# Linear attention with a relu-squared network behind it: other places in the period for the last attention group of even periods, and for some steps of odd and even periods

## Chip, core and metric

The kernel runs on one core of a Trainium2 chip. The metric is the device time of one execution in microseconds (us); of several runs the median counts. The matmul engine is TensorE (PE, its weight loads PEld), the others are VectorE (DVE), ScalarE (ACT) and GpSimd (POOL); SyncE (SP) issues the DMAs.

## What is computed

The input has 4 batches of 8 heads, 768 steps and 48 dimensions. Per head a delta rule runs over the steps, and the 8 heads side by side then pass a two-layer network:

```python
for t in range(S):
    kt, vt, bt = (k_n[:, :, t], v[:, :, t], beta[:, :, t, None])
    y[:, :, t] = np.einsum('bhd,bhde->bhe', q[:, :, t], state)
    v_old = np.einsum('bhde,bhd->bhe', state, kt)
    state = state + bt[:, :, :, None] * np.einsum('bhd,bhe->bhde', kt, vt - v_old)
...
x = np.ascontiguousarray(attn_out.transpose(0, 2, 1, 3)).reshape(B * S, H * D)
h = np.maximum(x @ w_in, 0.0)
return (h * h @ w_out)
```

`k_n` is k divided by its norm; `w_in` is 384 x 2048 and `w_out` 2048 x 384. All is float32.

## The kernel before

The 768 steps are cut into 12 units of 64 (`units`), for all 32 heads at once. Within a unit the recurrence becomes matmuls: products of the keys, the inverse of a triangular matrix of 32 x 32 (`invert`, 31 steps on DVE of two instructions each, L505 and L507), and products with the state that one unit hands to the next. The inverse is made for two units at a time, a pair. The network (`moe`) of unit u - 1 runs while the attention of unit u does; such a stretch is a period, here numbered by u. In the trace, periods 1 to 11 follow a prologue of some 100 us, in which the weights are loaded and split into a high and a low part; after period 11 comes the rest of the last network.

What PE does in a period, by lines:

- the network: 16 groups of nine matmuls of the first layer (L751, tile h), and 16 groups of six of the second (L735, tile o), with three transposes twice ahead of them (L711). After two groups of L751, ACT takes the relu, the square and a rounded copy (L758, L759, L761), and DVE takes the rest of that rounding (L726, tile h_l), which the L735 of the same columns read two steps later.
- `key_products` (L403): only in odd periods, for the next pair. ACT and DVE copy the result out (L415, L418, L420) by the letters of `copies`, per pair: A is ACT, D is DVE, B is both. `prepare` on DVE follows (L438 to L480, with POOL's L450 and L451 between), then the first steps of `invert`.
- `state_part` and `query_products`: L661 with L623 behind it; then L671 with L677; then L689 with L696, the period's last group. ACT copies w out of L677's result (L680), and L689 and L696 read w. POOL masks the result of L623 (L629). After L696, ACT copies y (L699), which the next period's L711 read.
- `below_both`: only in even periods, L593 with L594, then L605 with L606. They read what DVE makes of the finished inverse (`ended`: L525, L530, L532).

A matmul instruction of attention with float32 operands stands in the trace as two: 32 in the program are x64 in the trace.

The order is written out by hand. In each period `weave` takes the pieces of all these generators, each with a place from 0 to 1 out of the table `A`, sorts them by place and lets each issue its instructions, which every engine then runs in that order. `steps` places the attention groups (in even periods: L661, L593, L605, L671, L689; in odd ones: L403, L661, L671, L689), `inverse`, `ended` and `prepare` place DVE's work, `keys`, `queries`, `values` and `rows` place DMA loads and what follows each of them. The 31 pieces of the network stand evenly between `m0` and `m1`, and the rest of the last network's pieces (`end`, `out`) begins the next period. `first` is the number of inverse steps in an odd period; the rest falls to the even one. Tables under a period's number (2, 6, 8, 10) replace single rows of the even table for that period. And where two attention groups would touch, a piece of the network is drawn between them, while the period still has one:

```python
            gen, quiet = order.pop(0)
            if quiet is False and not apart and (filler[0], None) in order:
                order.remove((filler[0], None))
                next(filler[0], None)
            next(gen, None)
            if quiet is not True:
                apart = quiet is None
```

Of the kernel before, what the change touches and what calls it, by code (L numbers as in the profile page):

```python
# [20 lines left out]
def kernel(  # L21
# [43 lines left out]
     10: {'steps': [0.277, 0.4012, 0.4602, 0.5125, 0.5471]},  # L65
     'abs': 35,
     'ahead': 13,
     'copies': {0: 'AADA', 1: 'AADD', 2: 'ABDD'},
     'e0': 6,
     'e1': 2,  # L70
     'early': [0, 0],
     'even': {'end': 0.0,
              'ended': [0.2208, 0.2284, 0.2344, 0.2744],
              'inverse': [0.0404, 0.2141],
              'keys': [0.3956, 0.4523],
              'm0': 0.0,
              'm1': 0.5432,
              'out': 0.1098,
              'queries': [0.4923, 0.7603],
              'rows': [0.9979],  # L80
              'steps': [0.277, 0.4212, 0.4802, 0.5325, 0.5671],
              'values': [0.0128, 0.6834]},
     'f0': 0,
     'fill': [0, 0, 3, 0, 0, 1, 2, 0, 0, 1, 0, 0, 0, 0, 0, 0, 1, 0, 0, 2, 0, 0, 0, 1, 0, 0, 0, 0, 0, 0, 0, 0, 1, 0, 0, 0, 0,
              0, 0, 0, 1, 0, 0, 6, 5, 2, 1, 3, 5, 2, 3],
     'first': 11,
     'first1': 10,
     'kk': 0,
     'last': [2, 1],
     'low': 3,  # L90
     'mode': 'tttttttttttttttdd',
     'odd': {'end': 0.0,
             'inverse': [0.4412, 0.881],
             'keys': [0.0236, 0.172],
             'm0': 0.0,
             'm1': 0.8088,
             'out': 0.4224,
             'prepare': [0.3136, 0.3577],
             'queries': [0.4506, 0.8586],
             'rows': [0.9393],  # L100
             'steps': [0.2904, 0.4345, 0.7374, 0.8997],
             'values': [0.5395000000000001, 0.7395]},
     'order': '-01TABABAPPl2PBPPxPPPIIIGyZIIIIIIIIIIIIeeeecccVbbss',
     'over': 3,
     'plain': [('k', 3)]}
# [378 lines left out]
    def invert(d):  # L484
        need(("prepared", d["pair"]))
        lt, z = d["lt"], d["z"]
        if d["pair"] < FAST:
            lt = d["l16"]
            z = z.rearrange("p s t -> p (s t)")[:, :HB * QB].rearrange("p (h s t) -> p h s t", h=2, s=QB)
            tmp_ = apool.tile([P, 256], F32, name="tmp")  # L490
            for s in range(QB - 1):
                nj, nt = s + 1, QB - 1 - s
                tmp = tmp_[:, :2 * nj * nt].rearrange("p (h j t) -> p h j t", h=2, t=nt)
                nc.vector.tensor_tensor(out=tmp, op=ALU.mult, in0=lt[:, :, s:s + 1, s + 1:].broadcast_to([P, 2, nj, nt]),
                                        in1=z[:, :, :nj, s:s + 1].broadcast_to([P, 2, nj, nt]))
                nc.vector.tensor_tensor(out=z[:, :, :nj, s + 1:], in0=z[:, :, :nj, s + 1:], in1=tmp, op=ALU.subtract)
                if s == QB - 2:
                    done.add(("inverted", d["pair"]))
                yield
            return  # L500
        tmp_ = apool.tile([P, 256], F32, name="tmp")
        for s in range(HB - 1):
            nj, nt = s + 1, HB - 1 - s
            tmp = tmp_[:, :nj * nt].rearrange("p (j t) -> p j t", t=nt)
            nc.vector.tensor_tensor(out=tmp, op=ALU.mult, in0=lt[:, s:s + 1, s + 1:].broadcast_to([P, nj, nt]),  # L505
                                    in1=z[:, :nj, s:s + 1].broadcast_to([P, nj, nt]))
            nc.vector.tensor_tensor(out=z[:, :nj, s + 1:], in0=z[:, :nj, s + 1:], in1=tmp, op=ALU.subtract)  # L507
            if s == HB - 2:
                done.add(("inverted", d["pair"]))
            yield  # L510
# [363 lines left out]
    with tc.manual_schedule(engines=engines):  # L874
# [41 lines left out]
        inverse = invert(pair0)  # L916
# [16 lines left out]
        for u in range(1, A.get("stop", units)):  # L933
# [18 lines left out]
            if u % 2:  # L952
                kk = [iter(())] * 2
                if nxt:
                    inverse = invert(nxt)
# [47 lines left out]
```

## Time and profile before

| | us |
|---|---|
| median of 3 runs | 620.88 (619.26 to 621.07) |
| the profiled execution's own time | 621.46 |
| its span, first to last instruction | 619.4 |
| PE busy | 579.1 |
| DVE busy | 421.7 |
| ACT busy | 321.6 |
| POOL busy | 51.4 |

The profile is that of one execution. Busy time counts instructions, not waits; the ends of matmuls are modelled, so that the starts tell more than the ends. A wait is written behind the instruction that ended it, with who released it; "issue" is a wait for nothing that the profile shows. The chain of waits is the work that ended last, followed back from the end. A row of order of time gives start, duration, engine, line, tiles and count; a row of a stretch gives its bounds, its length and the busy time of each engine with its instructions, then the granted share of PE's clock.

### The profile page before, as it was taken

How to read it: one execution, taken by the hardware profiler on the slowest of the kernel's cores; microseconds unless marked ns; L12 is line 12 of the kernel's file. 1: busy time of each engine (PE TensorE's matmuls, PEld its weight loads, DVE VectorE, ACT ScalarE, POOL GpSimd, SP SyncE). 2: the span in 40 equal slices, each digit the busy share in tenths (PEclk: the TensorE clock that was granted, in tenths of full speed). 3: DMA queues.
4: the chain of work that ended last, by engine and by line, in shares of the span. 5: the costliest groups of instructions: out<-in, count | busy, mean ns of one | idle time of the engine just before them, and what ended most of it. 6: DMA issues, size and time to landing. Idle time of an engine off the chain costs nothing.

```text
span 619.4 us, 23429 instructions
## 1 busy us (share of the span) xinstructions
PE 579.1 (93%) x10616; PEld 550.5 (89%) x10616; DVE 421.7 (68%) x758; ACT 321.6 (52%) x507; POOL 51.4 (8%) x62
## 2 busy tenths in 40 slices
PE   5077899999999999999999999999999999999997
PEld 5055678999989999999999999999999999999997
DVE  3975989999934989845989557989349897412111
ACT  4345868645455545546544655454655455454442
POOL 3110000110100200200201001102002002001000
PEclk9568999999999999999999999999999999999999
DMA  8996070005025114045041243060252140110101
GB/s 250 273 282 197 6 124 7 4 1 93 14 41 90 31 29 76 5 70 87 3 83 23 28 80 53 3 104 3 38 82 40 28 79 3 29 27 2 28 1 25
DMA packets 146675, 37.79 MB, mean 61 GB/s; under 512 B 140272, under 2 KB 143344, under 8 KB 146576
## 3 DMA queue, kind: packets, MB, share of 16 engines
q1 hardware_dynamic: 146496, 36.20, 28.7%
q8 instruction: 83, 1.36, 0.9%
q14 instruction: 16, 0.13, 0.1%
q10 hardware_dynamic: 80, 0.10, 0.0%
HBM read 31.56 MB, written 4.72 MB: 59 GB/s over the span
## 4 chain that ended last, share of the span: by engine, by line
PE 84%; DVE 4%; SPq 4%; DMA 3%; issue 2%; ACT 2%; ACTq 0%
PE h L751 31%; PE o L735 29%; SPq L211 2%; PE o L237 2%; PE g L735 2%; PE g L237 2%; SPq L320 2%; PE g L671 2%; PE g L696 2%; PE g L677 2%; DMA kb<-in_q_dram 2%; PE g L661 2%; PE g L403 2%; PE g L623 2%; PE g L689 1%
## 5 line engine op out<-in xcount | busy, mean ns | idle before, releaser
L735 PE MATMUL o<-w,h_h 128*128 128x384 f32 x704 | 185.4, 344 | 0.0
L751 PE MATMUL h<-x_h,w 128*128 128x256 f32 x1152 | 170.3, 283 | 0.6 <-ACT x_h L713 0.6
L751 PEld LDWEIGHTS h<-x_h,w 128*128 128x128 f32 x1152 | 154.7, 190 | 1.5 <-ACT x_h L713 0.8
L726 DVE TENSOR_TENSOR h_l<-r,h_h 128x512 fp32r<-128x512 f32 x96 | 65.2, 684 | 102.1 <-ACT h_h L761 102.1
L735 PEld LDWEIGHTS o<-w,h_h 128*128 128x128 f32 x704 | 121.4, 189 | 2.7 <-issue 0.7
L758 ACT ACTIVATE r<-h 128x512 f32<-128x512 f32 x96 | 57.4, 598 | 120.7 <-PE h L751 102.2
L735 PE MATMUL o<-w,h_l 128*128 128x384 f32 x352 | 118.3, 336 | 0.0
L751 PE MATMUL h<-x_l,w 128*128 128x256 f32 x576 | 100.1, 283 | 0.0
L751 PEld LDWEIGHTS h<-x_l,w 128*128 128x128 f32 x576 | 82.5, 191 | 0.0
L735 PEld LDWEIGHTS o<-w,h_l 128*128 128x128 f32 x352 | 66.1, 188 | 0.0
L759 ACT ACTIVATE r<-r 128x512 f32<-128x512 f32 x96 | 60.8, 633 | 3.1
L761 ACT CAST h_h<-r 128x512 fp32r<-128x512 f32 x96 | 59.6, 621 | 3.0
L507 DVE TENSOR_TENSOR z<-z,tmp 128x31 f32<-128x31 f32 (+15 forms) x155 | 53.1, 343 | 5.3
L505 DVE TENSOR_TENSOR tmp<-lt,z 128x31 f32<-128x31 f32 (+15 forms) x155 | 52.5, 339 | 3.7
L629 POOL TENSOR_SCALAR_AFFINE_SELECT ap<-ap 64x1024 f32<-64x1024 f32 x24 | 32.7, 1364 | 246.5 <-ACT ap L626 227.9
L692 DVE TENSOR_TENSOR state<-state,g 48x768 f32<-48x768 f32 x22 | 20.9, 950 | 18.2 <-PE g L689 18.0
L699 ACT COPY y<-g 128x768 f32<-128x768 f32 x12 | 9.6, 799 | 40.2 <-PE g L696 40.2
L450 POOL MEMSET z<- 128x1024 f32 x5 | 4.8, 959 | 245.3 <-DVE lt L438 245.3
L714 DVE TENSOR_TENSOR x_l<-h,x_h 128x384 fp32r<-128x384 f32 x24 | 13.4, 557 | 13.7 <-ACT x_h L713 13.3
L713 ACT CAST x_h<-h 128x384 fp32r<-128x384 f32 x24 | 11.5, 479 | 20.1 <-PE h L711 20.1
L371 PE MATMUL g<-eye,tt 128*128 128x128 f32 x16 | 3.9, 424 | 17.5 <-DMA tt<-in_k_dram 16.3
L371 PEld LDWEIGHTS g<-eye,tt 128*128 128x128 f32 x16 | 3.1, 222 | 18.0 <-issue 16.4
(160 smaller groups left out, 804.0 us busy)
## 6 DMA issues: line engine op xcount, KB each, us to landing
w<-in_moe_w_out_dram SPq DMA_DIRECT2D x8, 768.0 KB, 8.4
w<-in_moe_w_in_dram SPq DMA_DIRECT2D x6, 768.0 KB, 6.8
vt<-in_v_dram SPq DMA_DIRECT2D x48, 96.0 KB, 3.2
kp<-in_k_dram SPq DMA_DIRECT2D x48, 96.0 KB, 3.3
out_dram<-rest SPq DMA_DIRECT2D x47, 96.0 KB, 2.2
kb<-in_q_dram SPq DMA_DIRECT2D x40, 64.0 KB, 2.7
kb<-in_k_dram SPq DMA_DIRECT2D x32, 64.0 KB, 2.8
w<-in_moe_w_in_dram SPq DMA_DIRECT2D x3, 512.0 KB, 8.3
```

Source lines behind the costliest of these rows:

```text
L237: nc.tensor.matmul(ps[:, c], lhsT=i, rhs=z.rearrange("p (c n) -> p c n", c=2)[:, c], start=(m == 0), stop=(m == len(terms) - 1))
L505: nc.vector.tensor_tensor(out=tmp, op=ALU.mult, in0=lt[:, s:s + 1, s + 1:].broadcast_to([P, nj, nt]), in1=z[:, :nj, s:s + 1].broadcast_to( ...
L507: nc.vector.tensor_tensor(out=z[:, :nj, s + 1:], in0=z[:, :nj, s + 1:], in1=tmp, op=ALU.subtract)
L629: nc.gpsimd.affine_select(out=half, in_=half, pattern=[[0, 2 * X], [1, C]], base=0, channel_multiplier=-1, compare_op=ALU.is_gt, fill=0.0)
L692: nc.vector.tensor_tensor(out=s[dims(j)], in0=s[dims(j)], in1=ps[dims(j)], op=ALU.add)
L714: nc.vector.tensor_tensor(out=x_l[:, :, cols], in0=xt, in1=x_h[:, :, cols].bitcast(F32), op=ALU.subtract)
L726: nc.vector.tensor_tensor(out=h_l, in0=r, in1=h_h.bitcast(F32), op=ALU.subtract)
L735: nc.tensor.matmul(o[i], lhsT=a[:, e, i * P:(i + 1) * P], rhs=w_[w], start=(ft == 0 and n == 0), stop=(ft == FT - 1 and n == 2))
L751: nc.tensor.matmul(hp[:, e], lhsT=half_of(("wi", kt, part))[w][:, f], rhs=x[:, kt], start=(n == 0), stop=(n == 3 * KT - 1))
L758: nc.scalar.activation(out=r, in_=hp, func=AF.Relu)
L759: nc.scalar.activation(out=r, in_=r, func=AF.Square)
L761: nc.scalar.copy(out=h_h, in_=r)
```

## The change

Only numbers of the table `A` change. The core of the diff, without the rows whose order in the program is shown below or stays as it was:

```diff
-     'copies': {0: 'AADA', 1: 'AADD', 2: 'ABDD'},
+     'copies': {0: 'AAAA', 1: 'AADD', 2: 'AADD'},
...
-              'm1': 0.5432,
+              'm1': 0.5244,
...
-              'steps': [0.277, 0.4212, 0.4802, 0.5325, 0.5671],
+              'steps': [0.2753, 0.398, 0.457, 0.5093, 0.6681],
...
-     'first': 11,
+     'first': 12,
...
-             'steps': [0.2904, 0.4345, 0.7374, 0.8997],
-             'values': [0.5395000000000001, 0.7395]},
+             'steps': [0.3088, 0.5641, 0.7558, 0.9181],
+             'values': [0.2314, 0.4823]},
```

The number 0.6681 for the last group of even periods holds for period 4 alone, since periods 2, 6, 8 and 10 have `steps` of their own, which stay. In period 4 no piece of the network is left to stand at the added distance, and the order on PE around that group stays: L677, six L735, L689. What does move PE's work in the other even periods is `m1`, which draws the network's pieces forward past places that stay.

In the order of PE, in period 6 from the end of L606 to the last group, before:

```order
L735 MATMUL o<-w_1267,h_l 128x384
L671 MATMUL g<-state,qt 64x48 x32
L677 MATMUL g<-vt,tt 64x48 x32
L735 MATMUL o<-w_1418,h_h 128x384 x2
L735 MATMUL o<-w_1418,h_l 128x384
L735 MATMUL o<-w_1418,h_h 128x384 x2
L735 MATMUL o<-w_1418,h_l 128x384
L689 MATMUL g<-w,kp 48x48 x32
L696 MATMUL g<-w,ap 64x48 x32
```

The same place now:

```order
L735 MATMUL o<-w_1267,h_l 128x384
L735 MATMUL o<-w_1418,h_h 128x384 x2
L735 MATMUL o<-w_1418,h_l 128x384
L735 MATMUL o<-w_1418,h_h 128x384 x2
L735 MATMUL o<-w_1418,h_l 128x384
L671 MATMUL g<-state,qt 64x48 x32
L677 MATMUL g<-vt,tt 64x48 x32
L689 MATMUL g<-w,kp 48x48 x32
L696 MATMUL g<-w,ap 64x48 x32
```

The six L735 with w_1418 moved ahead of L671, and L689 follows L677 directly. Period 8 has the same change.

In the order of PE, in period 10 at the same group, before:

```order
L671 MATMUL g<-state,qt 64x48 x32
L677 MATMUL g<-vt,tt 64x48 x32
L735 MATMUL o<-w_1267,h_h 128x384 x2
L735 MATMUL o<-w_1267,h_l 128x384
L735 MATMUL o<-w_1267,h_h 128x384 x2
L735 MATMUL o<-w_1267,h_l 128x384
L735 MATMUL o<-w_1418,h_h 128x384 x2
L735 MATMUL o<-w_1418,h_l 128x384
L735 MATMUL o<-w_1418,h_h 128x384 x2
L735 MATMUL o<-w_1418,h_l 128x384
L689 MATMUL g<-w,kp 48x48 x32
```

The same place now:

```order
L735 MATMUL o<-w_1267,h_h 128x384 x2
L735 MATMUL o<-w_1267,h_l 128x384
L671 MATMUL g<-state,qt 64x48 x32
L677 MATMUL g<-vt,tt 64x48 x32
L735 MATMUL o<-w_1418,h_h 128x384 x2
L735 MATMUL o<-w_1418,h_l 128x384
L735 MATMUL o<-w_1418,h_h 128x384 x2
L735 MATMUL o<-w_1418,h_l 128x384
L689 MATMUL g<-w,kp 48x48 x32
```

One group of six L735 (w_1267) moved from behind L677 to ahead of L671; the other six stay.

In the order of PE, in period 8 at the end of the first-layer group ahead of L593, before:

```order
L751 MATMUL h<-x_l,w_1285 128x256
L751 MATMUL h<-x_l,w_1314 128x256
L751 MATMUL h<-x_l,w_1347 128x256
L593 MATMUL g<-tt,mt 32x32
L594 MATMUL g<-t_6567,mt 32x32
```

The same place now:

```order
L751 MATMUL h<-x_l,w_1347 128x256
L751 MATMUL h<-x_h,w_1285 128x256
L751 MATMUL h<-x_h,w_1314 128x256
L751 MATMUL h<-x_h,w_1347 128x256
L751 MATMUL h<-x_h,w_1285 128x256
L751 MATMUL h<-x_h,w_1314 128x256
L751 MATMUL h<-x_h,w_1347 128x256
L751 MATMUL h<-x_l,w_1285 128x256
L751 MATMUL h<-x_l,w_1314 128x256
L751 MATMUL h<-x_l,w_1347 128x256
L593 MATMUL g<-tt,mt 32x32
L594 MATMUL g<-t_6564,mt 32x32
```

One group of nine L751 more stands ahead of L593. Period 10 has the same change, in period 6 L593 comes one group of L735 later, and in period 4 it comes one group earlier.

In odd periods 3, 5, 7 and 9, L403 comes one group of L751 later, L661 with L623 come five groups later, L671 with L677 one group later, so that twelve L735 instead of eighteen stand between L677 and L689. The loads of v and the DVE step behind them (L644) come earlier in odd periods; in periods 4, 6 and 8 the loads of k and q and the transposes behind them (L382) come some three to four groups earlier. Of the copies behind L403, the two on ACT and two on DVE of letter B (L415) become three on ACT (L418, L420) in these periods, and in the first pair three copies (L418, L420) go from DVE to ACT. Each odd period has one step of the inverse (L505, L507) more on DVE, each even one from period 4 on one less.

More of the change, by code (lines that the diff above doesn't have):

```diff
@@ L71 @@
      'early': [0, 0],
[L72 to L76, printed above, removed]
-              'm1': 0.5432,
+     'even': {'end': 0.0348,
+              'ended': [0.2238, 0.2284, 0.2612, 0.2744],
+              'inverse': [0.0457, 0.2194],
+              'keys': [0.3243, 0.3832],
+              'm0': 0.0062,
+              'm1': 0.5244,
               'out': 0.1098,
-              'queries': [0.4923, 0.7603],
+              'queries': [0.4108, 0.7603],
               'rows': [0.9979],
-              'steps': [0.277, 0.4212, 0.4802, 0.5325, 0.5671],
+              'steps': [0.2753, 0.398, 0.457, 0.5093, 0.6681],
               'values': [0.0128, 0.6834]},
@@ L91 @@
      'mode': 'tttttttttttttttdd',
-     'odd': {'end': 0.0,
-             'inverse': [0.4412, 0.881],
-             'keys': [0.0236, 0.172],
+     'odd': {'end': 0.0022,
+             'inverse': [0.4563, 0.881],
+             'keys': [0.0776, 0.172],
              'm0': 0.0,
@@ L98 @@
              'prepare': [0.3136, 0.3577],
-             'queries': [0.4506, 0.8586],
+             'queries': [0.4445, 0.8789],
              'rows': [0.9393],
-             'steps': [0.2904, 0.4345, 0.7374, 0.8997],
-             'values': [0.5395000000000001, 0.7395]},
+             'steps': [0.3088, 0.5641, 0.7558, 0.9181],
+             'values': [0.2314, 0.4823]},
      'order': '-01TABABAPPl2PBPPxPPPIIIGyZIIIIIIIIIIIIeeeecccVbbss',
```

## Prediction

> **What bounds the kernel now.** The page first, for the span and the engines' totals; then busy time by stretches; then who kept the matmul engine waiting; then the matmul engine's own order of time at the places that the change touches. The table by stretches has the time of each, then the busy time of PE, PEld, DVE, ACT and POOL with their instructions.
>
> ```profile
> span 619.4 us, 23429 instructions
> ...
> PE 579.1 (93%) x10616; PEld 550.5 (89%) x10616; DVE 421.7 (68%) x758; ACT 321.6 (52%) x507; POOL 51.4 (8%) x62
> ...
> 140.00:575.00 435.00, 432.65 (x7961) 420.51 (x7960) 302.14 (x550) 222.78 (x349) 36.85 (x28) 1.00 0.27 44
> ```
>
> From 140 to 575 us, in periods 2 to 11, PE is busy 432.65 of 435.00 us at full clock. What other engines gain there is worth nothing unless PE waits for it; what adds a wait to PE, or takes one away, is worth just that. Of its waits after the first 105 us, these are where the change reaches, with total, times and longest:
>
> ```profile
> PE g L696 <- issue: 1.4, 4, 0.5
> ...
> PE g L594 <- DVE t L532: 0.5, 2, 0.2
> ```
>
> The first row is the even periods' last group; "issue" means that no semaphore held PE. Here is period 6 from L677 on, then the break in periods 8 and 10, and an odd period's group without one:
>
> ```profile
> 355.09 1.11 PE L677 MATMUL g<-vt,tt 64*64 64x48 f32 x64
> 356.13 0.62 PE L735 MATMUL o<-w,h_h 128*128 128x384 f32 x2
> ...
> 357.38 0.94 PE L689 MATMUL g<-w,kp 64*48 64x48 f32 x64
> 358.13 0.69 PE L696 MATMUL g<-w,ap 64*64 64x48 f32 x33
> 359.04 0.68 PE L696 MATMUL g<-w,ap 64*64 64x48 f32 x31 [0.22 <-issue]
> 359.65 0.62 PE L735 MATMUL o<-w,h_h 128*128 128x384 f32 x2
> ...
> 444.20 0.62 PE L735 MATMUL o<-w,h_h 128*128 128x384 f32 x2
> ...
> 446.21 0.88 PE L696 MATMUL g<-w,ap 64*64 64x48 f32 x48
> 447.62 0.45 PE L696 MATMUL g<-w,ap 64*64 64x48 f32 x16 [0.53 <-issue]
> 448.00 0.62 PE L735 MATMUL o<-w,h_h 128*128 128x384 f32 x2
> ...
> 530.50 1.11 PE L677 MATMUL g<-vt,tt 64*64 64x48 f32 x64
> ...
> 534.59 1.11 PE L696 MATMUL g<-w,ap 64*64 64x48 f32 x63
> 536.14 0.20 PE L696 MATMUL g<-w,ap 64*64 64x48 f32 x1 [0.45 <-issue]
> 536.27 0.62 PE L735 MATMUL o<-w,h_h 128*128 128x384 f32 x2
> ...
> 401.89 1.11 PE L696 MATMUL g<-w,ap 64*64 64x48 f32 x64
> 402.94 0.45 PE L735 MATMUL o<-w,h_h 128*128 128x384 f32 x1
> ```
>
> Starts tell the cost, since the ends of matmuls are modelled. L696 takes 402.94 - 401.89 = 1.05 us undisturbed, and 1.52, 1.79 and 1.68 in periods 6, 8 and 10: breaks of 0.47, 0.74 and 0.63 us, after the 33rd, 48th and 63rd matmul. That regular step says what they are. Queue and stretches from break to break:
>
> ```profile
> q8 instruction: 83, 1.36, 0.9%
> ...
> 359.04:447.62 88.58, 87.81 (x1659) 85.31 (x1659) 65.61 (x120) 45.30 (x71) 7.86 (x6) 1.00 0.29 47
> 447.62:536.14 88.52, 87.84 (x1659) 85.19 (x1659) 64.09 (x118) 45.30 (x71) 8.14 (x6) 1.00 0.25 43
> ```
>
> 83 packets of 16 KB carry PE's 2 x 10616 instructions: a packet, a block of code, is 256 of them, or 128 matmuls with their weights. From break to break there are 1659 matmuls both times; 13 blocks are 1664, and the queue's waits fill the rest. So the breaks stand at block ends: the next block is not there yet. A block ends 128 matmuls after the last. In period 6 that is 33 of L696, 64 of L689, six of L735 and 25 of L677, so it began at about 356.13 - 25 x 0.016 = 355.7 us and the next came 3.3 us later; in period 8 (48 + 64 + 6 + 10) it began at 444.0 and the next came 3.6 us later. I take 3.3 to 3.6 us as the time that a block must last.
>
> **The change part by part.** *Periods 6 and 8: L689 right behind L677.* The upper bound `m1` moves six L735 matmuls from between the two groups to before L671. L689 reads w, which ACT copies out of L677's result:
>
> ```profile
> 352.98 0.51 PE L735 MATMUL o<-w,h_h 128*128 128x384 f32 x2
> ...
> 353.50 0.51 PE L735 MATMUL o<-w,h_h 128*128 128x384 f32 x2
> ...
> 356.27 0.80 ACT L680 COPY w<-g 128x768 f32<-128x768 f32 x1 [1.71 <-PE g L677]
> ...
> 429.95 2.01 DVE L532 STREAM_TRANSPOSE t<-z 128x1024 f32<-128x1024 f32 x1
> ...
> 432.02 0.21 PE L594 MATMUL g<-t,mt 32*32 32x32 f32 x1 [0.24 <-DVE t L532]
> ```
>
> The copy ends at 357.07, and a matmul follows a semaphore by some 0.06 us (L532 ends at 431.96, L594 starts at 432.02). So L689 can start at about 357.13 instead of 357.38: the slot after L677 shrinks from 1.25 to 1.00 us. The six matmuls still cost 1.04 us elsewhere (three per 353.50 - 352.98 = 0.52). Net +0.79 us a period, +1.6 us for both. ACT is free there (it had idled 1.71 us), so no more is queued ahead of the copy.
>
> *The blocks in periods 6 and 8.* The block now holds six more of L677 in the place of the six L735: by the slots it lasts 31 x 0.016 + 1.00 + 0.75 + 33 x 0.016 = 2.8 us without a break, where it lasted 0.4 + 1.25 + 0.75 + 0.5 = 2.9. The break grows by 0.1 to 0.2 each if the fetch takes as long: +0.3 for both. Bounds: both breaks gone (-1.2 us), or a fetch slower by 0.3 us each (+0.9). The q loads (L338) leave this place, which speaks for the lower half, but period 10 broke without such loads behind it.
>
> *Period 10.* Between L677 and L689 stand six L735 instead of twelve. The break after 63 means that this block began with L689, and the one before it 12 L735, 64 L677 and some 50 of L671 earlier, at 529.7: two blocks in 6.4 us, both short. If both fetches bind, losing six L735 lengthens the break by their full 1.04 us; if only the last does, by nothing. I take +0.6, 0 to 1.04 for the range.
>
> *Periods 8 and 10: L593/L594 nine matmuls later.* First the stretch of this group in period 8, then in period 6, where nothing waits, and from the chain of waits what 54 L751 take:
>
> ```profile
> 431.53:433.22 1.69, 1.45 (x130) 1.00 0.05 10
> ...
> 344.94:346.16 1.22, 1.22 (x130) 1.00 0.05 13
> ...
> 143.63 6.47 PE h L751 x54
> ```
>
> The wait for L532 costs 1.69 - 1.22 = 0.47 us, and it comes twice by the table of waits. One group of nine L751 (6.47 / 6 = 1.08 us) now stands ahead, and `first` takes one inverse step off these periods' DVE. Both waits go: -0.9 us. Period 4's group comes nine matmuls earlier, but there the step saved on DVE covers it; 0 to +0.3.
>
> *Odd periods: L403 one group later, L661/L623 five later, L415 gone.* PE's counts and switches stay the same. At risk is the L735 group that reads h_l of L726, queued on DVE behind L454 to L480:
>
> ```profile
> 387.15 2.35 POOL L629 TENSOR_SCALAR_AFFINE_SELECT ap<-ap 64x1024 f32<-64x1024 f32 x2 [0.64 <-ACT ap L626]
> ...
> 387.42 0.91 DVE L463 TENSOR_TENSOR bt<-betas,s 128x32 f32<-128x32 f32 x1
> 388.36 1.17 DVE L464 TENSOR_TENSOR bt<-bt,s 128x32 f32<-128x32 f32 x1
> 390.71 0.69 DVE L726 TENSOR_TENSOR h_l<-r,h_h 128x512 fp32r<-128x512 f32 x1
> ...
> 391.81 0.34 PE L735 MATMUL o<-w,h_l 128*128 128x384 f32 x1
> ...
> L463 DVE TENSOR_TENSOR bt<-betas,s x6: 191/906/907, 23.2 to 475.8; 128x32 f32<-128x32 f32 x6
> ```
>
> L726 ends 0.4 us before it is read. L403 comes one group of 1.08 us later against it, and DVE has two copies (some 1.4 us) less while ACT starts its copies behind the relu chain; left alone that is a wait of about 0.2 us in each of four periods. But L463 takes 0.191 us where POOL is still and 0.91 beside L629, and L464 likewise. L629 follows L623, which moves behind them, so DVE gains about 1.7 us before L726 and the wait does not come: 0, with +0.8 as the other end. The Trainium skill's page "SBUF — State Buffer", section "SBUF: two separate sides", says that GpSimd and a DVE instruction with two SBUF inputs hold the shared port pair in turn, for a whole instruction. The trace agrees (0.191 against 0.91); by that rule the term is 0. The block that ends in an odd L696 keeps twelve of its eighteen L735: 2.1 + 0.75 + two halves of 0.5 = 3.8 us, above 3.6; 0, at most +0.2 each.
>
> *The first pair's copy, DVE to ACT.* Three ACT copies of some 0.6 us stand ahead of L441, so this pair's inverse ends about 0.7 us later. PE uses it late:
>
> ```profile
> 42.90 1.92 DVE L532 STREAM_TRANSPOSE t<-lt 128x1024 f32<-128x1024 f32 x1
> ...
> 48.55 1.29 PE L545 MATMUL g<-t,vt 32*32 32x32 f32 x128
> ```
>
> L545 starts 3.7 us after L532 ends, so 0; without that cover +0.7. All other moved DVE, ACT and SP work (k, q and v loads, L382, L644) lies beside busy PE: 0.
>
> **The sum.** +1.6 + 0.3 + 0.6 - 0.9 = +1.6 us. The profiled execution took 621.46 us, its span of 619.4 and 2.06 around it, so it would take 623.1. The median of the runs is 620.88; on that, **622.5 us**, 0.26% more. About 0.3%, 1.9 us, is what a measurement of this kernel can tell from no change.
>
> **The rivals.** *All block ends bind fully (0.22):* blocks arrive at the slow end in periods 6 and 8 (+0.9), period 10 pays its full 1.04 and the odd periods some 0.5: 1.6 + 0.9 + 1.04 + 0.5 - 0.9 = +3.1, 624.0 us, slower. For it: 0.74 us in period 8. It decides from 3.8 us a block on. *Blocks come sooner (0.10):* with the q loads gone the breaks of 6, 8 and 10 vanish, -1.84; with +1.6 - 0.9 that is -1.1, 619.7 us. Against it: period 10. *Code fetch has no part (0.13):* the breaks belong to the groups and stay; 1.6 - 0.9 = +0.7, 621.6 us. Against it stand the steps of 15. The Trainium skill's page "Runtime: NRT & Kernel Launch", section "Instruction fetch mechanics", calls the refill in 256-instruction blocks mostly hidden, since dispatch is slower than it. The trace agrees on the block and not on the hiding (0.74 us); by that rule the block terms are 0. *The forecast (0.55):* +0.5 to +2.8.
>
> **How the numbers follow.** Of the forecast's 0.55 some two fifths lie above +1.9, and nearly all of the first rival: slower 0.43. Faster needs the second rival and another microsecond: 0.06. No change: 0.51. The range takes the rivals' centres but the far end: -0.3 to +3.4, 620.6 to 624.3 us.
>
> **What would show it.** Right: in periods 6 and 8 a wait L689 <- ACT w of about 0.8 us; no wait L594 <- DVE; breaks in L696 still a multiple of 128 matmuls apart, period 10's the longest; no wait of L735 for h_l. Wrong: L696 without breaks in period 10, a new wait in an odd period, or L689 starting later than 1.1 us after L677's last matmul.

## The result, and the profile after

The changed kernel takes 624.46 us (median of 14 runs, 622.22 to 625.67), the kernel before beside it 621.35 (617.93 to 624.64): ratio 1.0051, 95% interval 1.0034 to 1.0069, so 3.2 us slower. A second set of runs gave 1.0061 (1.0034 to 1.0087). The forecast on the median was +1.6, or 622.5 us, its range up to +3.4, or 624.3 us; on the profiled executions (624.18 against 621.46) it is +2.7.

The page of the changed kernel and its table of waits (total, times, longest):

```profile
span 622.5 us, 23433 instructions
...
PE 578.7 (93%) x10616; PEld 548.7 (88%) x10616; DVE 411.8 (66%) x747; ACT 325.7 (52%) x514; POOL 50.5 (8%) x62
```

```profile
PE g L689 <- ACT w L680: 1.8, 2, 0.9
PE g L696 <- issue: 1.6, 3, 1.0
PE o L735 <- issue: 0.6, 1, 0.6
...
PE h L751 <- DVE x_l L714: 0.6, 3, 0.2
PE h L751 <- ACT rest L796: 0.5, 1, 0.5
```

PE is as busy as before (578.7 against 579.1). The wait of L594 for t is gone, and the wait of L689 for w has come, as forecast. The last two rows were not forecast: L751, a period's first layer, waits at the start of periods 4, 6, 8 and 10 (in period 10 the table names L796, but there too L751 follows the first L714, 0.15 us after its end). Their place in order of time on PE: period 6's last group, the start of period 8, and period 10's last group.

```profile
356.00 1.11 PE L677 MATMUL g<-vt,tt 64*64 64x48 f32 x64
358.04 0.94 PE L689 MATMUL g<-w,kp 64*48 64x48 f32 x64 [0.92 <-ACT w L680]
358.79 0.68 PE L696 MATMUL g<-w,ap 64*64 64x48 f32 x33
...
404.92 0.49 PE L711 MATMUL h<-eye,y 128*128 128x128 f32 x3
...
407.54 0.34 PE L735 MATMUL o<-w,h_l 128*128 128x384 f32 x1
408.06 0.35 PE L751 MATMUL h<-x_h,w 128*128 128x256 f32 x1 [0.18 <-DVE x_l L714]
...
537.04 1.11 PE L696 MATMUL g<-w,ap 64*64 64x48 f32 x62
539.11 0.25 PE L696 MATMUL g<-w,ap 64*64 64x48 f32 x1 [0.96 <-issue]
```

From L677 to L689 it is 358.04 - 356.00 = 2.04 us; before it was 2.29 with six L735 (1.04 us) in it. So 0.79 us is lost, the forecast's number. In period 8, L751 starts 0.52 us after the last L735, where one matmul follows another by 0.17; with the next matmul the loss is 0.42, the same in periods 4 and 6, and 0.78 in period 10: 2.0 us together.

What this L751 waits for is not x_l itself. It reads x_h, and writes tile h, which has two buffers (`bufs=2` of `ps_h`). The two groups of L711 have filled both, and L714 is the last to read each. The wait ends with the first of the two L714 (in period 8 at 407.91 us, L751 follows at 408.06). The L751 that read x_l start at 408.84, after the second L714 has ended at 408.37. "Wait for x_l" below means this wait for L714.

A ledger of the profile, from PE's starts (what a start comes later than usual behind the same line): w 2 x 0.79 = 1.58; x_l 2.04; t 0.83 less; the pauses marked issue 3.63 instead of 3.11. That is +3.3 in all; the stretch from period 2's first L711 to the end grew from 478.7 to 482.3. When each profile's own sums are taken off its stretch, 474.7 to 475.5 us are left in all 20 profiles of this study: PE's own work hardly changes, its waits and pauses do. Below, a kernel's profile is told as these sums. A profile is one execution and not always near its median, so that sums and times can differ, by up to 2.8 us in these runs.

### The profile page after: what moved, and what is told of

The parts are those of the page before. It is cut to its first block, busy times and chain, and to the rows that moved or that the text cites. A ratio compares the mean times of both kernels' runs of the same rounds, so it can differ in the third digit from the quotient of the medians.

```text
span 622.5 us, 23433 instructions
## 1 busy us (share of the span) xinstructions
PE 578.7 (93%) x10616; PEld 548.7 (88%) x10616; DVE 411.8 (66%) x747; ACT 325.7 (52%) x514; POOL 50.5 (8%) x62
## 4 chain that ended last, share of the span: by engine, by line
PE 88%; SPq 4%; DMA 3%; ACT 2%; issue 2%; DVE 0%; ACTq 0%
PE h L751 34%; PE o L735 30%; PE o L237 2%; SPq L211 2%; PE g L735 2%; PE g L237 2%; SPq L320 2%; PE g L671 2%; PE g L661 2%; DMA kb<-in_q_dram 2%; PE g L677 2%; PE g L696 2%; PE g L623 2%; PE g L403 2%; PE g L689 1%
## 5 line engine op out<-in xcount | busy, mean ns | idle before, releaser
L735 PE MATMUL o<-w,h_h 128*128 128x384 f32 x704 | 185.2, 344 | 0.0
L751 PE MATMUL h<-x_h,w 128*128 128x256 f32 x1152 | 170.7, 284 | 1.7 <-ACT x_h L713 0.6
L751 PEld LDWEIGHTS h<-x_h,w 128*128 128x128 f32 x1152 | 154.2, 190 | 4.3 <-issue 1.9
L726 DVE TENSOR_TENSOR h_l<-r,h_h 128x512 fp32r<-128x512 f32 x96 | 65.3, 685 | 108.7 <-ACT h_h L761 108.6
L758 ACT ACTIVATE r<-h 128x512 f32<-128x512 f32 x96 | 57.4, 598 | 128.0 <-PE h L751 115.7
L735 PEld LDWEIGHTS o<-w,h_h 128*128 128x128 f32 x704 | 121.3, 188 | 2.8 <-issue 0.8
L735 PE MATMUL o<-w,h_l 128*128 128x384 f32 x352 | 118.3, 336 | 0.6 <-issue 0.6
L751 PE MATMUL h<-x_l,w 128*128 128x256 f32 x576 | 100.2, 283 | 0.0
L751 PEld LDWEIGHTS h<-x_l,w 128*128 128x128 f32 x576 | 82.6, 191 | 0.0
L735 PEld LDWEIGHTS o<-w,h_l 128*128 128x128 f32 x352 | 66.1, 188 | 0.0
L761 ACT CAST h_h<-r 128x512 fp32r<-128x512 f32 x96 | 59.6, 620 | 3.0
L507 DVE TENSOR_TENSOR z<-z,tmp 128x31 f32<-128x31 f32 (+15 forms) x155 | 56.9, 367 | 5.3
L505 DVE TENSOR_TENSOR tmp<-lt,z 128x31 f32<-128x31 f32 (+15 forms) x155 | 56.4, 364 | 3.7
L629 POOL TENSOR_SCALAR_AFFINE_SELECT ap<-ap 64x1024 f32<-64x1024 f32 x24 | 31.9, 1331 | 247.7 <-ACT ap L626 231.5
L692 DVE TENSOR_TENSOR state<-state,g 48x768 f32<-48x768 f32 x22 | 20.8, 944 | 21.7 <-PE g L689 21.6
L418 DVE COPY mt<-g 128x512 f32<-128x512 f32 x10 | 6.9, 690 | 21.0 <-ACT z L420 20.8
L714 DVE TENSOR_TENSOR x_l<-h,x_h 128x384 fp32r<-128x384 f32 x24 | 12.8, 555 | 9.6 <-ACT x_h L713 8.9
```

The source lines that it names most:

```text
L629: nc.gpsimd.affine_select(out=half, in_=half, pattern=[[0, 2 * X], [1, C]], base=0, channel_multiplier=-1, compare_op=ALU.is_gt, fill=0.0)
L692: nc.vector.tensor_tensor(out=s[dims(j)], in0=s[dims(j)], in1=ps[dims(j)], op=ALU.add)
L714: nc.vector.tensor_tensor(out=x_l[:, :, cols], in0=xt, in1=x_h[:, :, cols].bitcast(F32), op=ALU.subtract)
L726: nc.vector.tensor_tensor(out=h_l, in0=r, in1=h_h.bitcast(F32), op=ALU.subtract)
L735: nc.tensor.matmul(o[i], lhsT=a[:, e, i * P:(i + 1) * P], rhs=w_[w], start=(ft == 0 and n == 0), stop=(ft == FT - 1 and n == 2))
L751: nc.tensor.matmul(hp[:, e], lhsT=half_of(("wi", kt, part))[w][:, f], rhs=x[:, kt], start=(n == 0), stop=(n == 3 * KT - 1))
```

## The experiments

In the expectations, S1, S2 and S3 are the groups of L661, L671 and L689, and BL1 is L593 with L594.

Theory 1: the twelfth step of odd periods (`first`) makes x_l late. Theory 2: the place of L382 does. Rival: the moved attention steps of odd periods do.

**One step fewer, or L382 ahead of the last step.**

```diff
-     'first': 12,
+     'first': 11,
```

> The changed kernel with 'first' 11 again: the even pairs' inverse has one step fewer in the odd periods, and L382 still stands behind all of them. Theory 1 (VectorE has one step too many at the end of odd periods, so that L382, both L692 and both L714 run back to back and L751 of the next period waits 0.35, 0.42, 0.42 and 0.78 us for x_l of L714): all four waits go, about 2.0 us less than the changed kernel, 622.4 us. Theory 2 (it is L382 behind the last step that makes L714 late, not the number of steps): the waits shrink by a part only, 623.4 to 624.2. Rival (the moved S1, S2 and L629 of odd periods make VectorE late): the waits stay, 624.4 +- 0.4. The waits of L689 for w of L680 (two of 0.92) and the pause of L735 in period 8 (0.8) stay under all three.

621.87 us, ratio 1.0024 (1.0002 to 1.0046). No wait for x_l. But 0.44 for t in period 4 is back, L735 waits once for h_l (0.70), and the pauses are 4.45.

```diff
-             'queries': [0.4445, 0.8789],
+             'queries': [0.4506, 0.8586],
```

> The changed kernel with the odd periods' 'queries' at 0.4506 and 0.8586 again: L382 stands ahead of the twelfth step instead of behind it, twelve steps as before. Theory 1 (one step too many): VectorE has the same work up to L714, so the waits of L751 for x_l of L714 stay (together 2.0 us), 624.4 +- 0.4. Theory 2 (the place of L382): the waits of L751 go, 622.4. Rival (S1, S2, L629 of odd periods): the waits stay, 624.4 +- 0.4.

622.32, ratio 1.0041 (1.0019 to 1.0063): the waits shrink from 0.42 to 0.35 in periods 4, 6 and 8 and from 0.78 to 0.36 in period 10. Theory 2 is a small part at most.

**The odd periods' places back, then L403's alone.**

```diff
-             'steps': [0.3088, 0.5641, 0.7558, 0.9181],
-             'values': [0.2314, 0.4823]},
+             'steps': [0.2904, 0.4345, 0.7374, 0.8997],
+             'values': [0.5395000000000001, 0.7395]},
```

> The changed kernel with the odd periods' 'steps' and 'values' as before: S1, S2, S3 and the value tiles stand where they stood, twelve steps and L382 behind them stay. Theory 3 (a ledger at the end of odd periods: before, VectorE was idle for 0.28 and 0.84 us ahead of the two L714, 1.12 in all; the twelfth step costs 0.82, the moved S1, S2 and value work about 0.85; each alone fits, both together don't): no wait of L751 for x_l, or one under 0.15 us, since L382 behind the last step makes it tight; two waits of L689 for w (0.92) stay: about 2.0 us less than the changed kernel if nothing comes out elsewhere, +1.2 against before; +3.2 if it does. Theory 1 (the twelfth step by itself): the waits stay, +3.2.

619.66, ratio 1.0006 (0.9988 to 1.0024): no wait for x_l, with twelve steps. So theory 1 falls as the only cause. First the slack at the end of period 7 in the kernel before, where L714 waits for ScalarE twice:

```profile
402.94 1.91 DVE L692 TENSOR_TENSOR state<-state,g 48x768 f32<-48x768 f32 x2
405.13 0.56 DVE L714 TENSOR_TENSOR x_l<-h,x_h 128x384 fp32r<-128x384 f32 x1 [0.28 <-ACT x_h L713]
406.53 0.56 DVE L714 TENSOR_TENSOR x_l<-h,x_h 128x384 fp32r<-128x384 f32 x1 [0.84 <-ACT x_h L713]
```

VectorE at the same place, of the changed kernel and of this one (whose next period's first L711 starts at 403.97):

```profile
383.23 2.07 DVE L438 STREAM_TRANSPOSE lt<-z 128x1024 f32<-128x1024 f32 x1
...
404.28 1.25 DVE L382 STREAM_TRANSPOSE qt<-kb 128x1024 f32<-128x1024 f32 x1
405.45 1.87 DVE L692 TENSOR_TENSOR state<-state,g 48x768 f32<-48x768 f32 x2
407.35 1.02 DVE L714 TENSOR_TENSOR x_l<-h,x_h 128x384 fp32r<-128x384 f32 x2
```

```profile
380.54 2.04 DVE L438 STREAM_TRANSPOSE lt<-z 128x1024 f32<-128x1024 f32 x1
...
401.61 1.24 DVE L382 STREAM_TRANSPOSE qt<-kb 128x1024 f32<-128x1024 f32 x1
402.77 1.88 DVE L692 TENSOR_TENSOR state<-state,g 48x768 f32<-48x768 f32 x2
405.01 0.56 DVE L714 TENSOR_TENSOR x_l<-h,x_h 128x384 fp32r<-128x384 f32 x1 [0.36 <-ACT x_h L713]
406.41 0.56 DVE L714 TENSOR_TENSOR x_l<-h,x_h 128x384 fp32r<-128x384 f32 x1 [0.84 <-ACT x_h L713]
```

Read each start against its next period's first L711 (404.92 and 403.97). L438, the first step behind the copies of L403's result, comes 21.69 us ahead in the changed kernel and 23.43 here, 1.74 later; L692 comes 0.53 behind and 1.20 ahead, 1.73 later. What is lost at L438 arrives whole at the end: between them VectorE has no idle time over 0.15 us in either (in period 10 of the changed kernel L382 waits 0.35). With the slack (0.36 and 0.84) L714 waits for ScalarE, without it PE waits for L714.

Of the 1.74 us, 1.06 are L403's own place (29.71 us ahead of the next L711 instead of 30.77). The rest, 0.69, comes from ScalarE, which now makes relu, square and rounding (L758 to L761) between L403 and its copies. In the changed kernel its first copy starts 1.92 us after L403 starts:

```profile
375.21 2.10 PE L403 MATMUL g<-kt 48*64 48x64 f32 x128
376.61 0.62 ACT L761 CAST h_h<-r 128x512 fp32r<-128x512 f32 x1
377.13 0.58 ACT L418 COPY z<-g 128x512 f32<-128x512 f32 x1
```

In this one it starts 1.23 us after:

```profile
373.20 2.10 PE L403 MATMUL g<-kt 48*64 48x64 f32 x128
374.43 0.58 ACT L418 COPY z<-g 128x512 f32<-128x512 f32 x1 [2.35 <-PE g L403]
```

```diff
-             'steps': [0.3088, 0.5641, 0.7558, 0.9181],
+             'steps': [0.2904, 0.5641, 0.7558, 0.9181],
```

> The changed kernel with only the first of the odd periods' 'steps' at 0.2904 again: L403 stands one group of nine L751 earlier, all else as changed. Theory (VectorE has no idle time from L438 to L692, so what L403 loses is carried to the period's end): L438 starts 23.4 and L692 1.2 us ahead of the next period's first L711 (changed kernel: 21.7 ahead, 0.5 behind), no wait of L751 for x_l, two waits of L689 for w stay: about 2.0 to 2.8 us less than the changed kernel, within 1.5 us of before. Rival (L661, L671, L689 and the value work delay VectorE): the waits for x_l stay, 3 us above before.

620.66, ratio 1.0008 (0.9990 to 1.0026); L438 comes 23.44 and L692 1.10 ahead, no wait for x_l. So of the odd periods' moved places it is L403's, nine L751 later, and not the other steps or the value work.

**Parts on the kernel before.**

```diff
-     'first': 11,
+     'first': 12,
```

> The kernel before with nothing but 'first' 12: the even pairs' inverse has one step more in odd periods 3, 5, 7, 9 and one fewer in the even ones. L382 stands ahead of the last step. Theory 1 (one step too many on VectorE at the end of odd periods): L751 waits for x_l of L714 by 0.28 us in each of periods 4, 6, 8, 10, as in the changed kernel with L382 put ahead of the last step: +1.1; the waits of L594 for t of L532 (0.8 together in periods 8 and 10) stay or shrink, since the inverse ends sooner by one step: together -0.8 to +1.1, 618.5 to 620.4. Rival (the step counts only with the moved S1, S2 and L629 of the changed kernel): no wait of L751 for x_l, 618.5 to 619.3.

619.08, ratio 0.9991 (0.9972 to 1.0009): no wait for x_l, against theory 1 once more, and none for t. L692 comes 0.13 ahead instead of 1.15: the step takes 1.02 of the slack, which does not use it up. In the changed kernel, then, the late L403 and the twelfth step are both needed for the wait.

```diff
-     'first': 11,
+     'first': 12,
...
-             'steps': [0.2904, 0.4345, 0.7374, 0.8997],
-             'values': [0.5395000000000001, 0.7395]},
+             'steps': [0.3088, 0.5641, 0.7558, 0.9181],
+             'values': [0.2314, 0.4823]},
```

> The kernel before with two parts of the change alone: 'first' 12, and the odd periods' 'steps' and 'values' of the changed kernel (S1, S2, S3 and the value tiles at their new places). Theory 3 (ledger): the waits of L751 for x_l of L714 in periods 4, 6, 8 and 10 are here, 0.28 us each as in the changed kernel with L382 ahead of the last step, though the even periods are as before; no wait of L594 for t; 619.4 to 620.5 where before has 619.4. Rival (even periods of the changed kernel have part in it): no waits of L751, as with 'first' 12 alone.

625.02, ratio 1.0085 (1.0056 to 1.0114). The waits for x_l come as expected, and a dearer one with them, in all four odd periods:

```profile
PE o L735 <- DVE h_l L726: 3.7, 4, 0.9
PE h L751 <- DVE x_l L714: 1.3, 4, 0.3
```

Here VectorE still makes the copies of letter B, two L415 of 0.70 us. L438 and the L726 behind it come 1.40 us later after L403 than in the changed kernel. So the changed `copies` are what keeps the wait for h_l away.

```diff
-     'copies': {0: 'AADA', 1: 'AADD', 2: 'ABDD'},
+     'copies': {0: 'AAAA', 1: 'AADD', 2: 'AADD'},
```

> The kernel before with nothing but the new 'copies' (the first pair's copies to ScalarE). The prediction puts it at 0.0 within -0.6 to +0.7; the profile of the changed kernel starts its first L711 after 130 us 0.56 us sooner than before. Theory (the prologue waits for its loads): -0.3 to +0.3 in the time. Rival (ScalarE does the copies sooner or later than VectorE): 0.6 us either way, with the first L711 that much sooner or later.

618.42, ratio 0.9983 (0.9959 to 1.0007): no clear change. L438 comes 1.41 us sooner, 23.42 ahead of the period's end, and L692 0.72 sooner. What does this are the later pairs' copies, which the same row of the table changes; the first pair's were not tried alone. First L711 comes at 137.5 to 141.7 us over the profiles, so the 0.56 us there says nothing.

**The direct neighbours.**

```diff
-              'm1': 0.5244,
+              'm1': 0.5432,
```

> The changed kernel with 'm1' of even periods at 0.5432 again: in periods 6 and 8 one group of six L735 stands between L677 and L689, in 4 and 10 two groups. If the direct neighbourhood of L677 and L689 is what costs 1.6 us (two waits for w of L680), and the pause of L735 in period 8 (0.8) and the longer pause of L696 in period 10 (0.6 over the kernel before) hang on the place of L735 and L696 in the order, these 3.0 us go: about 621.4; the four waits of L751 for x_l of L714 (2.0) stay. If only the waits of L689 go and the pauses come back elsewhere: 622.9. If the neighbourhood costs nothing of its own (the time comes out in the next wait): 624.4 +- 0.3.

619.86, ratio 0.9997 (0.9977 to 1.0018): no wait for w, pauses 2.52, waits for x_l as before (2.27).

```diff
-              'm1': 0.5432,
+              'm1': 0.5244,
```

> The kernel before with nothing but 'm1' of even periods at 0.5244: the direct neighbourhood alone. In periods 6 and 8 L689 follows L677 directly. Theory (neighbourhood costs by itself): two waits of L689 for w of L680 of 0.92 us, +1.6; pauses marked issue change by -0.3 to +1.5; no wait of L751 for x_l of L714, since odd periods are as before: 620.9 to 622.3 where before has 619.25 (+1.6 to +3.1). Rival (the cost arises only together with the other moved places): the waits of L689 are under 0.3 us, time within 0.5 us of before.

622.82, ratio 1.0037 (1.0017 to 1.0056): three waits for w of 0.9 (period 4 has become one of them), two for h_l (0.70 each), none for t. The neighbourhood costs by itself.

**The pauses marked issue.**

```diff
+        def extra():
+            ps = ps_h.tile([P, bank], F32, name="h")[:, :P]
+            for _ in range(16):
+                nc.tensor.matmul(ps, lhsT=ident, rhs=ident, start=True, stop=True)
...
-                "T": beginning, "Z": zeros, "-": lambda: None}
+                "T": beginning, "Z": zeros, "-": extra}
```

> The kernel before with 16 more f32 matmuls of 128x128 (32 pairs of weight load and matmul on TensorE) in the prologue, into a tile that nobody reads; nothing else is changed. Theory (the pauses of L696 marked issue lie where TensorE enters a new stretch of 256 instructions, every 128 matmuls): the pauses move by 32 matmuls: those after the 33rd, 48th and 63rd L696 of a group in periods 6, 8 and 10 come after the 1st, 16th and 31st, and the one of period 4 (after the 18th) leaves the group; time about as before, +0.0 to +0.6 us. Rival (the pauses belong to this group of matmuls, to its tiles or to what it waits for): they stay at their places, and the time is as before.

622.72, ratio 1.0044 (1.0021 to 1.0067). Periods 6 and 8:

```profile
355.75 0.22 PE L696 MATMUL g<-w,ap 64*64 64x48 f32 x1
356.17 1.15 PE L696 MATMUL g<-w,ap 64*64 64x48 f32 x63 [0.20 <-issue]
...
444.68 0.41 PE L696 MATMUL g<-w,ap 64*64 64x48 f32 x16
445.86 0.92 PE L696 MATMUL g<-w,ap 64*64 64x48 f32 x48 [0.76 <-issue]
```

After the 1st and the 16th, as expected, and period 4's stands in L689; but period 10's left the group (one of 0.88 stands ahead of it, in an L751 at 526.25 us). Counted from the program's start, the pauses stand behind matmul 4808, 6467 and 8126, as before, whatever instruction is there: they belong to the blocks. The time was missed: the pauses come to 4.44 instead of 3.11.

The traces show the blocks' arrival as well. Each packet of the queue q8 is a block of code. In the kernel before, packets end at 357.62, 446.29 and 534.77 us, and L696 goes on 1.43, 1.33 and 1.37 us later, at 359.04, 447.62 and 536.14. In the 20 profiles, 99 starts of PE after 105 us come over 0.16 us late with no semaphore to hold them; 98 of them lie 1.2 to 1.6 us after the end of such a packet, where only 6% of all of PE's starts lie. No two packets there start less than 3.25 us apart, which is near the 3.3 to 3.6 us that the prediction took for a block.

**A version that beats both.** Whether twelve L735 between L677 and L689 end the pauses was tried first, with BL1 (L593, L594) later as the change has it:

```diff
-     6: {'steps': [0.277, 0.4212, 0.4952, 0.5325, 0.5671]},
-     8: {'steps': [0.277, 0.4062, 0.4802, 0.5325, 0.5671]},
-     10: {'steps': [0.277, 0.4012, 0.4602, 0.5125, 0.5471]},
+     6: {'steps': [0.277, 0.4212, 0.4952, 0.5145, 0.5671]},
+     8: {'steps': [0.277, 0.4212, 0.4802, 0.5145, 0.5671]},
+     10: {'steps': [0.277, 0.4162, 0.4602, 0.5125, 0.5471]},
```

> The kernel before with two places of its own: BL1 nine L751 later in periods 8 and 10 (the gain of the change without the rest), and L671/L677 one group of six L735 earlier in periods 6 and 8, so that twelve L735 and not six stand between L677 and L689: really further apart. Theory (a stretch of 256 instructions must last about 3.5 us; six L735 more in the stretch that ends in L696 take the pauses of 0.43 and 0.74 away): -0.8 and -1.2, 617.3. Rival (the pauses go elsewhere or stay): -0.8 alone, 618.4. Rival 2 (L671 so early waits for L606 or for its tiles): L671 waits, 619 to 620.

619.87, ratio 0.9997 (0.9976 to 1.0017): period 8's pause stands in L677 now, one block earlier (1.08), and L677 waits once for tt of L608 (0.59). Then parts were put back in the changed kernel, first these three:

```diff
-              'm1': 0.5244,
+              'm1': 0.5432,
...
-     'first': 12,
+     'first': 11,
...
-             'queries': [0.4445, 0.8789],
+             'queries': [0.4506, 0.8586],
```

> The changed kernel with 'm1' of even periods, 'first' and 'queries' of odd periods as before: no direct neighbours in periods 6 and 8, eleven steps, L382 ahead of the last; what is left of the change are BL1 nine L751 later in periods 8 and 10, the first pair's copies, the places of loads, and S1, S2, L629 of odd periods. Theory (neighbourhood and late x_l are the whole loss, BL1 the gain): no wait of L689 or of L751, one gain of 0.8: 618.4 (-0.8 against before). Rival (waits removed come out in the next ones, as when 'first' alone was put back): 619.3 to 620.3.

621.87, ratio 1.0043 (1.0021 to 1.0065), with eleven steps: three waits for t (1.31), pauses 3.44. The loss is larger than these rows show; the profiled execution, 619.11 us, is the shortest of the twelve. With twelve steps and the odd periods' places back (the run c_mix):

```diff
-              'm1': 0.5244,
+              'm1': 0.5432,
...
-             'queries': [0.4445, 0.8789],
+             'queries': [0.4506, 0.8586],
-             'steps': [0.3088, 0.5641, 0.7558, 0.9181],
-             'values': [0.2314, 0.4823]},
+             'steps': [0.2904, 0.4345, 0.7374, 0.8997],
+             'values': [0.5395000000000001, 0.7395]},
```

> The changed kernel with 'm1' of even periods and 'queries', 'steps' and 'values' of odd ones as before: no direct neighbours, twelve steps in odd periods with the old places of S1, S2, S3 and L382; what is left of the change are 'first' 12, the copies and the places of the moves inside even periods. By the ledger no wait of L751 for x_l, none of L594 for t, none of L689 for w: only the pauses marked issue are left, some 2.5 to 3.5 us in all as in the kernel before (3.1): -0.8 to -0.5 against before, as with 'first' 12 alone (-0.6). Rival (what is freed comes out in longer pauses): +-0.3 of before.

619.46 and, a second time, 618.82: ratios 0.9991 (0.9967 to 1.0015) and 0.9986 (0.9961 to 1.0010). No wait for w, x_l or t is left. The same with the copies as before, so that `first` 12 and the small moves inside the periods remain (the run c_mixcopies):

```diff
-     'copies': {0: 'AAAA', 1: 'AADD', 2: 'AADD'},
+     'copies': {0: 'AADA', 1: 'AADD', 2: 'ABDD'},
```

> The kernel of the run c_mix with the first pair's copies as before as well. If the copies are worth 1.0 us (as b_copies alone at 0.9983 says): 1.0 us above c_mix. If they are worth nothing (the prediction's term of 0.0): the same as c_mix within 0.6 us.

618.78, ratio 0.9980 (0.9953 to 1.0007), so the copies are worth nothing that shows there.

> The kernel of c_mixcopies once more. If its pauses stay as in the kernel before (3.1 us) and only the two waits for t (0.83) are gone: 0.9987 of before. If they stay as short as in its first profile (1.8 us): 0.9965. If pauses take the gain back: 0.9995 to 1.0005.

617.82, 0.9961 (0.9941 to 0.9981), and the same kernel once more, beside the same runs of before, 618.78, 0.9977 (0.9956 to 0.9999): 1.4 to 2.4 us faster than before, though the first set alone left no change open. Its three profiles have pauses of 1.76, 2.09 and 0.63 us at block ends; the last is of the shortest of its twelve executions (616.36 us). All waits of PE in that one after 105 us:

```profile
PE h L751 <- ACT x_h L713: 0.6, 1, 0.6
PE g L606 <- issue: 0.5, 1, 0.5
```

The pauses' lengths differ between executions of one program; the changed kernel's second profile says the same:

> The changed kernel once more, on one chip with the next two. Waits of L689 for w (two of 0.92) and of L751 for x_l (0.18, 0.18, 0.18, 0.55) come back to the hundredth, since they hang on instructions alone. If the pauses marked issue are set by the program alone, they come back within 0.1 us too (0.38 and 0.23 and 0.96 of L696, 0.64 of L735); if the fetch of the next block varies from execution to execution, they differ by 0.2 to 0.5 us at the same matmuls. Time: +3.2 against before (1.0051), within 0.0018 of it.

```profile
540.51 0.31 PE L696 MATMUL g<-w,ap 64*64 64x48 f32 x2 [1.51 <-issue]
```

Period 10's pause is 1.72 instead of 1.17, and period 8's in L735 (0.80) is not there at all, while the waits for w come back to 0.01 and for x_l to 0.06. The packet ahead of period 10's pause shows where the difference comes from: it started 0.85 us after the first of the 128 matmuls ahead of the pause and took 0.93 us in the first profile, 1.19 and 1.31 us in the second.

## Why the prediction was wrong, point by point

- *Neighbours in periods 6 and 8, +1.6:* right, 1.58 in the profile.
- *L594's wait gone, -0.9:* right, 0.83.
- *Blocks as the cause of the pauses:* right, by the shift and by the packets' times. The Trainium skill's page "Runtime: NRT & Kernel Launch", section "Instruction fetch mechanics", calls the refill mostly hidden; here most of the some 70 block ends after 105 us have no pause, but one to eight in each profile do, 0.6 to 4.5 us in all. *Period 10, +0.6 of at most 1.04:* 0.51 in the changed kernel's first profile, 1.06 in its second. The pause averages 1.42 in the seven profiles with six L735 there (0.45 in the twelve with twelve that keep the blocks in place), so on the average nearly the full 1.04 is paid, and the term was too small. *Periods 6 and 8, +0.3:* period 6 had +0.16; period 8 1.24 instead of 0.74 in one profile, 0.51 in the other. Undecided, since the pauses vary by that much. *The block terms together, +0.9:* 0.52 and 0.43 in the two profiles. That the total is no farther off is partly luck: the sum says nothing of the pause of 0.40 in period 4, which is gone in both.
- *h_l in odd periods, 0:* right, and L463 and L464 took 0.19 us. But the copies carry it: without them it is four waits of 1.2 us. And the 1.7 us that VectorE gained there it paid again behind L726 (last section), so that they were no gain at the period's end.
- *The step that failed:* "All other moved DVE, ACT and SP work ... lies beside busy PE: 0", together with `first` counted only where it takes a step off. I followed L403's delay to the next read of h_l and stopped, and I did not add up VectorE's work to the end of the odd period. VectorE carried the delay (1.73) and the added step (0.84, from the run with eleven) to L714 at the period's end, where the slack had been 0.28 + 0.84 = 1.12; the copies gave back 0.72 on the kernel before. That makes 1.85; in the profile L692 comes 1.68 later than before. With either the step or L403 put back there is no wait; with both as changed there is: +2.04, on no line of the sum. The rival of block ends binding fully has the right total with the wrong cause: the pauses grew by 0.5, not by its 2.4.

The parts don't add in the times: `m1` back is worth 3.3 us and L403 back 2.7 of 3.2. In the profiles' stretches they are 2.7 and 2.4 of 3.6. With the 0.83 gained for t, that is 0.7 too much there, and 2.0 in the times. Each ratio is known to some 1.1 us, and the pauses differ by up to a microsecond between executions, which can cover it; whether it does is not shown.

## What to carry to other kernels

An in-order engine that is off the critical path has a balance up to its last reader in the period: carry each delay there, compare the sum with the slack read from its idle time ahead of that reader, and count a step that is shifted between two stages in both. Look also at the buffers that this reader frees: a matmul can wait for them before it needs the result. And a pause at the end of a code block is found by counting instructions from the program's start; its length needs several executions. The end of the code packet ahead of it tells whether the block was late.

## What was not expected of the hardware

- A block's arrival varies: the same pause was 1.17 and 1.72 us, another 0.80 and none, in two executions of one program, and the pauses end 1.2 to 1.6 us after the packet.
- A collision of VectorE with GpSimd moves rather than goes. The changed kernel's GpSimd and VectorE in period 7:

```profile
391.31 3.10 POOL L629 TENSOR_SCALAR_AFFINE_SELECT ap<-ap 64x1024 f32<-64x1024 f32 x2 [3.58 <-ACT ap L626]
```

```profile
388.66 0.19 DVE L463 TENSOR_TENSOR bt<-betas,s 128x32 f32<-128x32 f32 x1
...
392.12 1.15 DVE L505 TENSOR_TENSOR tmp<-lt,z 128x60 f32<-128x60 f32 x1
393.31 1.17 DVE L507 TENSOR_TENSOR z<-z,tmp 128x60 f32<-128x60 f32 x1
```

  L629 no longer meets L463 (0.19 us, 0.91 before), but a step of the inverse, whose two instructions take 0.22 us each where GpSimd is still (the run with the odd periods' places back). The two lose 1.88 us there. With L403 alone put back it is the next step, 1.18 and 1.17 us.
